# Attention of a fused attention and expert kernel laid out anew: pairs of heads staged side by side, 64x64 score products, one softmax instruction for four heads

## The chip, the cores and the metric

The kernel runs on one core of a Trainium2 chip. The core has five instruction queues that run side by side and each in its own order: TensorE (PE, matrix products and transposes through a product with the identity), VectorE (DVE), ScalarE (ACT), GpSimd (POOL) and SyncE (SP, which here only issues transfers). They wait for one another through semaphores. Transfers are carried out by 16 DMA engines. SBUF holds tiles of up to 128 partitions; PE writes to PSUM, and DVE or ACT copy from there ("eviction"). The metric is the device time of one execution in microseconds, the median over runs.

## What is computed

Banded attention with two masks, then a mixture of experts in which each token goes to one expert. Everything is float32.

```python
B, H, S, D = 8, 8, 576, 64
scores = q @ k.T / sqrt(D)                       # per batch and head, 576 x 576
rel = pos[:, None] - pos[None, :]
mask_plain = (rel >= 0) & (rel < 32)             # heads 0..3
mask_dil = (rel >= 0) & (rel < 128) & (rel % 4 == 0)   # heads 4..7
scores = where(mask, scores, -1e9)
attn = exp(scores - max) / (sum + 1e-9)
x = (attn @ v) as [4608 tokens, 512]
logits = x @ w_gate + modality_bias[modality_id]  # 8 experts
e = argmax(logits); gate = softmax(logits)[e]
out[token] = gate * (relu(x @ w1[e]) @ w2[e])     # w1 512 x 1024, w2 1024 x 512
```

## The kernel before

**Stages.** First the attention of all eight batches, with the routing of each batch worked in behind it; then the experts, in slots of 256 tokens of one expert. The change touches the attention alone.

**Units.** The attention is cut into tiles of 64 queries, which see 96 keys each. With the tokens of the dilated heads ordered by their class (position modulo 4), both masks are a band of 32 in that order, so both kinds of heads run through the same code: kind 0 are heads 0 to 3, kind 1 heads 4 to 7. A unit takes two tiles of one kind (the fifth unit of a batch one tile of each), that is, 2 tiles x 4 heads. A batch has 9 units and there are 72 in all, numbered t.

**One iteration of the loop.** The loop is software-pipelined, and PE, DVE, ACT and SP run it in the order in which it is written (`manual_schedule` over `MANUAL`); POOL's order is made by the scheduler. Iteration t emits:

1. `scores` of unit t: four products (lines 300 and 301). The queries of two heads lie as interleaved columns of `qT`, with zeros in the other head's 64 rows, so that one 128x128 by 128x96 product gives two heads of 64 queries. Then four times a DVE instruction (L305) that adds the mask and reduces the minimum (queries are stored negated, so the minimum is the maximum's negative; it shows as a custom instruction and a read of the accumulator), and four ACT exponentials (L308), with the minimum as the bias.
2. A piece of `qk_chunks` for keys of a coming half batch: four PE transposes (L257) of the loaded `kn` and two DVE evictions on 64 partitions each into `kT` (L272).
3. `attend` of unit t-2: eight PE products (L322) of the transposed probabilities `pT` and the values `vw`.
4. `logits` of unit t-4: small PE products (L360) of `uxh` and `uxl`, the two parts of the transposed output.
5. `normalize` of unit t-2 on DVE (L329, L330, L332, the last writing `x_sb`), and `gather_logits` of unit t-4 on DVE (L366, L371).
6. A piece of `qk_chunks` for queries: four PE transposes and two ACT evictions on 64 partitions into `qT` (L270).
7. `store` of unit t-3: two PE transposes of `x_sb` (L339), the ACT copy `uxh` (L343), the DVE difference `uxl` (L344), and the DMA of the rows to `x_dram` (L348, L352).
8. `probsT` of unit t-1: four PE transposes of the probabilities (L313), and the ACT eviction `pT` (L316).
9. One step of each task in `tasks`, above all the routing of the batch before (`gating`, from iteration 4 of the next batch on).

Pieces of step 2 and 6 come in eight of nine iterations of a batch: four for kind 0, four for kind 1.

**Routing on POOL.** `gating` uses POOL for small sums (L376 to L379, L416, L430, L432, L435, L437, operations on 96 partitions with at most 48 elements) and for six indirect DMAs per batch that scatter token numbers to the table of the experts (L442). From batch 6 on POOL also gathers rows of x for the first slots (L579), and for the first slot it computes six halves of the split of `w1` (L664).

**Loads.** SP issues the loads of a half batch (`load_qk`, then `load_v`) at iterations 0 and 4 of the batch before: keys and queries of four heads as 72 partitions with 8 successive tokens each, so that one packet has 2,048 bytes; values in packets of 256 bytes.

Of the kernel before, what the change touches and what calls it, by code (L numbers as in the profile page):

```python
# [10 lines left out]
F32 = mybir.dt.float32  # L11
# [14 lines left out]
NE = 8  # L26
# [7 lines left out]
SI = 8  # L34
PL = S // SI
# [26 lines left out]
def kernel(  # L62
# [21 lines left out]
    ps_s = ctx.enter_context(tc.tile_pool(name="ps_s", bufs=2, space=PSUM))  # L84
# [7 lines left out]
    # what the last batch's dilated units don't need lies where the experts can begin before those end  # L92
# [10 lines left out]
    for kd, pool in enumerate((aper0, aper)):  # L103
        qT.append(pool.tile([P, 2, S, 2], F32, name=f"qT{kd}"))
        kT.append(pool.tile([P, 2, WIN + S], F32, name=f"kT{kd}"))
    vw = [[pool.tile([KW, NTILE, 4, D + 1], F32, name=f"vw{kd}_{i}") for i, pool in enumerate((aperr, aper))] for kd in range(2)]

    def load_qk(b, kd):
        qn = ald.tile([PL, 4, SI, D], F32, name="qn")
        kn = ald.tile([PL, 4, SI, D], F32, name="kn")  # L110
        for g in (range(2) if b == 0 else (slice(0, 4),)):
            hs = g if isinstance(g, slice) else slice(2 * g, 2 * g + 2)
            for t, src in ((kn, k), (qn, q)):
                nc.sync.dma_start(out=t[:, hs], in_=src[b, 4 * kd + hs.start:4 * kd + hs.stop].rearrange("h (p si) d -> p h si d", si=SI))
# [25 lines left out]
    for kd in range(2):  # L140
        for a in range(2):
            (nc.gpsimd if kd else nc.vector).memset(qT[kd][a * D:(a + 1) * D, :, :, 1 - a], 0.0)
# [12 lines left out]
    # masks hold 0 where a key is seen and BIG elsewhere; rows are (query, head of the pair)  # L155
    MT = 6
    masks = cpool.tile([P, MT, KW], F32, name="masks")
    starts = [None, 0, CL - 2 * TQ, 2 * CL - 4 * TQ, 3 * CL - 6 * TQ, 3 * CL - 7 * TQ]
    nc.gpsimd.memset(masks, 0.0)
    for m, o in enumerate(starts):  # L160
        mt = masks[:, m, :]
        nc.gpsimd.affine_select(out=mt, in_=mt, pattern=[[2, KW]], compare_op=ALU.is_ge,
                                fill=BIG, base=-1, channel_multiplier=-1)
        nc.gpsimd.affine_select(out=mt, in_=mt, pattern=[[-2, KW]], compare_op=ALU.is_ge,
                                fill=BIG, base=2 * WIN, channel_multiplier=1)
        if o is not None:
            mo = masks[:, m, 0:WIN + o]
            nc.gpsimd.affine_select(out=mo, in_=mo, pattern=[[0, WIN + o]], compare_op=ALU.is_ge,
                                    fill=BIG, base=2 * o - 1, channel_multiplier=-1)
# [4 lines left out]
    # gate weights, modality terms, ids  # L174
# [20 lines left out]
    def constants():  # L195
        """What the routing needs, in pieces to be put between the first units."""
# [52 lines left out]
    def qk_chunks(kd, qn, kn):  # L249
        """The transposes of one half's keys and queries, as pieces to be put between units."""  # L250
        def chunk(h, is_q):
            src = qn if is_q else kn
            g, a = h // 2, h % 2
            pt = ps_t.tile([P, 512], F32, name="pt")
            ptv = pt[:, 0:4 * PL].rearrange("c (s p) -> c s p", p=PL)
            for s in range(4):
                nc.tensor.transpose(out=ptv[:, s, :], in_=src[:, h, 2 * s:2 * s + 2].rearrange("p u d -> p (u d)"),  # L257
# [642 lines left out]
```

## Time and profile before

| | |
|---|---|
| runs (three) | 791.31, 795.54, 800.52 us, median 795.54 |
| span of the profiled execution | 801.4 us, 5.9 us above the median of the runs |
| attention, normalisations of unit 0 to unit 71 | 23.3 to 336.4 us |
| mean granted TensorE clock | 0.940 |

The profile page gives the busy time of each engine, and groups of instructions by source line, with the mean duration of one and the idle time ahead of it with what ended it. The trace behind it answers further questions: the instructions in order of time, or the busy time of each engine between any two moments. "x4" in a row means that four like instructions were merged. A line number such as L305 is that of the kernel before; those of the changed kernel are 1 to 7 off, and each is given with its name.

### The profile page before, as it was taken

The page shows a single profiled execution, that of the slowest core. Times are in us where ns is not written, and L with a number is a line of the kernel's source. Part 1 is how long each engine was busy: PE and PEld are TensorE (multiplying, and loading weights), DVE is VectorE, ACT ScalarE, POOL GpSimd, SP SyncE. Part 2 cuts the span into 40 slices and gives each one's busy share as a digit, 9 for nine tenths or more (in the row PEclk, how much of TensorE's full clock was granted, in tenths as well). Part 3 has the DMA queues.
Part 4 walks back from the last instruction along what each step waited for, and adds up shares of the span by engine and source line. Part 5 has one row for each costly group of instructions (what it writes and reads, how often), then busy time and mean ns, then how long its engine had stood idle before and what let it go on. Part 6 is the DMA issues. An engine that isn't in the chain of part 4 may idle for free. (4 is left out here: it accounts for less than half of the span.)

```text
span 801.4 us, 16980 instructions
## 1 busy us (share of the span) xinstructions
PE 708.6 (88%) x5769; PEld 639.2 (80%) x5769; DVE 537.9 (67%) x1586; ACT 475.0 (59%) x933; POOL 350.6 (44%) x444
## 2 busy tenths in 40 slices
PE   7688888888882779999999988999999999699984
PEld 5688888888782768988889877988899999598963
DVE  5488888878883467687667744777666677457641
ACT  5588888788783349564366624656555456335641
POOL 5100314131235127577776524565556665156600
PEclk7799999999997579999999997999999999989998
DMA  8779777687836673102111261111111112611350
GB/s 164 166 173 179 163 140 143 148 150 155 146 81 142 159 178 79 40 2 54 55 28 47 75 194 53 46 47 48 51 54 54 41 41 89 191 51 53 115 155 24
DMA packets 97959, 79.63 MB, mean 99 GB/s; under 512 B 68443, under 2 KB 77707, under 8 KB 97870
## 3 DMA queue, kind: packets, MB, share of 16 engines
q1 hardware_dynamic: 88638, 59.32, 33.1%
q0 software_dynamic: 9232, 19.19, 8.4%
q8 instruction: 47, 0.77, 0.5%
q14 instruction: 42, 0.34, 0.2%
HBM read 122.15 MB, written 19.51 MB: 177 GB/s over the span
## 5 line engine op out<-in xcount | busy, mean ns | idle before, releaser
L579 POOL DMA_INDIRECT xg<-x_dram,gi x148 | 171.8, 1161 | 46.0 <-issue 39.7
L683 PE MATMUL pt<-xh,w1h 128*128 128x256 f32 x576 | 166.9, 290 | 10.6 <-ACT w1h L662 10.0
L683 PE MATMUL pt<-xh,w1l 128*128 128x256 f32 x576 | 167.4, 291 | 7.1 <-DVE w1l L664 7.1
L683 PE MATMUL pt<-xl,w1h 128*128 128x256 f32 x576 | 165.4, 287 | 0.0
L683 PEld LDWEIGHTS pt<-xh,w1h 128*128 128x128 f32 x576 | 113.1, 196 | 12.5 <-ACT w1h L662 10.6
L683 PEld LDWEIGHTS pt<-xh,w1l 128*128 128x128 f32 x576 | 112.8, 196 | 10.5 <-DVE w1l L664 10.3
L723 PE MATMUL po<-w2l,hh 128*128 128x512 f32 x296 | 117.6, 397 | 0.0
L723 PE MATMUL po<-w2h,hh 128*128 128x512 f32 x296 | 117.6, 397 | 0.0
L723 PE MATMUL po<-w2h,hl 128*128 128x512 f32 x296 | 117.4, 397 | 0.0
L674 ACT ACTIVATE hh<-pt 128x256 fp32r<-128x256 f32 x144 | 53.2, 383 | 108.2 <-PE pt L683 107.9
L270 ACT ACTIVATE qT<-pt 64x288 f32<-64x288 f32 x128 | 86.0, 672 | 51.4 <-PE pt L257 46.9
L683 PEld LDWEIGHTS pt<-xl,w1h 128*128 128x128 f32 x576 | 113.0, 196 | 0.8
L675 DVE SCALAR_TENSOR_TENSOR hl<-pt,hh 128x256 fp32r<-128x256 f32 x144 | 58.1, 421 | 78.8 <-ACT hh L674 78.6
L308 ACT ACTIVATE pe<-sm,nmx 128x96 f32<-128x96 f32 x288 | 84.6, 364 | 35.9 <-DVE nmx L305 35.1
L322 PE MATMUL po<-vw,pT 96*64 96x65 f32 x1152 | 75.4, 237 | 29.5 <-ACT pT L316 28.8
L664 DVE TENSOR_TENSOR w1l<-w1r,w1h 128x1024 fp32r<-128x1024 f32 (+1 forms) x74 | 85.0, 1204 | 20.6 <-ACT w1h L662 20.6
L322 PEld LDWEIGHTS po<-vw,pT 96*64 96x64 f32 x1152 | 65.2, 145 | 39.2 <-ACT pT L316 35.3
L272 DVE COPY kT<-pt 64x288 f32<-64x288 f32 x128 | 73.3, 572 | 28.4 <-PE pt L257 26.5
L662 ACT CAST w1h<-w1r 128x1024 fp32r<-128x1024 f32 (+1 forms) x80 | 76.9, 1003 | 21.1 <-DMA w1r<-in_moe_w_dram 11.4
L664 DVE TENSOR_TENSOR w2l<-w2r,w2h 128x1024 fp32r<-128x1024 f32 x76 | 88.6, 1220 | 0.6 <-ACT w2h L662 0.3
L300 PE MATMUL pss<-kT,qT 128*128 128x96 f32 x576 | 81.8, 288 | 1.3 <-ACT qT L270 1.3
L727 POOL DMA_INDIRECT out_dram<-ys,idt x37 | 39.1, 1056 | 91.6 <-issue 32.8
(175 smaller groups left out, 1224.2 us busy)
## 6 DMA issues: line engine op xcount, KB each, us to landing
w1r<-in_moe_w_dram SPq DMA_DIRECT2D x76, 512.0 KB
w2r<-in_moe_w_dram SPq DMA_DIRECT2D x76, 512.0 KB
kn<-in_k_dram SPq DMA_DIRECT2D x14, 576.0 KB
qn<-in_q_dram SPq DMA_DIRECT2D x14, 576.0 KB
vw<-in_v_dram SPq DMA_DIRECT2D x32, 192.0 KB
x_dram<-x_sb SPq DMA_DIRECT2D x40, 128.0 KB
vw<-in_v_dram SPq DMA_DIRECT2D x32, 96.0 KB
xg<-x_dram,gi POOLq DMA_INDIRECT x148, 3.3
```

Of the source, the lines that this page charges most:

```text
L270: nc.scalar.mul(dst, inp, -1.0 / 8.0)
L272: nc.vector.tensor_copy(out=dst, in_=inp)
L300: nc.tensor.matmul(out=ssv[:, j, :], lhsT=qT[kd][:, g, TQ * i:TQ * (i + 1), :].rearrange("p t a -> p (t a)"), rhs=kT[kd][:, g, TQ * i:TQ * ...
L308: nc.scalar.activation(out=self.pe[:, j, :], in_=sm[:, j, :], func=AF.Exp, bias=nmx[:, j:j + 1], scale=-1.0)
L322: nc.tensor.matmul(out=pov[u * TQ:(u + 1) * TQ, h, :], lhsT=self.pT[:, 2 * u + h // 2, h % 2::2], rhs=self.vts[kd][:, i, h, :], start=True ...
L579: load = nc.gpsimd.indirect_dma_start(out=xg[:, g, :], out_offset=None, in_=rows, in_offset=bass.IndirectOffsetOnAxis(ap=gi[:, g:g + 1], a ...
L662: (hi_eng.copy if hi_eng is nc.scalar else hi_eng.tensor_copy)(out=hi[cut], in_=raw[cut])
L664: lo_eng.tensor_tensor(out=lo[cut], in0=raw[cut], in1=hi[cut].bitcast(F32), op=ALU.subtract)
L674: nc.scalar.activation(out=hh[:, f, :], in_=ph, func=AF.Relu)
L675: nc.vector.scalar_tensor_tensor(out=hl[:, f, :], in0=ph, scalar=0.0, in1=hh[:, f, :].bitcast(F32), op0=ALU.max, op1=ALU.subtract)
L683: nc.tensor.matmul(out=ph, lhsT=wt[:, fs], rhs=xt[:, c, :], start=(c + n == 0), stop=(c + n == KC + 1))
L723: nc.tensor.matmul(out=py, lhsT=ht[:, f, ts_], rhs=wt[:, f % 2, :], start=(f + n == 0), stop=(f + n == FC + 1))
```

## The change

It rewrites how the attention's operands are staged, with the rest of the loop in its order:

- **Loads.** `load_qk` puts two heads side by side: partition p (48 of them per pair of heads, 96 for the two pairs) holds tokens 48 s + p, each as 64 numbers of one head beside 64 of the other. That makes eight DMAs per half batch in place of two, each of one head, in runs of 64 numbers (256 bytes). For kind 1 the class order is made here, by the load.
- **Transposes and evictions.** A piece now has three transposes of 96x128 in place of four of 72x128, and one eviction on 128 partitions of 2 x 144 elements, contiguous in the destination, in place of two on 64 partitions with strided destinations. Queries are evicted by ACT as before; keys of kind 0 by DVE, keys of kind 1 now by ACT.
- **Scores.** `qT` has no zeros and no interleaving any more. Eight products of 64 rows by 64 columns with 96 keys, each for one tile and one head, in place of four of 128x128. They go to the four quarters (two halves of the rows, two of the output's partitions) in turn, and to two banks of PSUM. The pool of these tiles has one buffer of two banks, in place of two of one bank.
- **Softmax.** One DVE addition of the mask for all four heads (384 elements per partition), one DVE maximum, one POOL subtraction of the maximum, one ACT exponential. Masks now hold the large negative number, five combinations of two tiles.
- **attend** reads the probabilities of each head as 128 successive columns, and alternates between the two tiles.

```diff
@@ load_qk
-        qn = ald.tile([PL, 4, SI, D], F32, name="qn")
-        kn = ald.tile([PL, 4, SI, D], F32, name="kn")
-        for g in (range(2) if b == 0 else (slice(0, 4),)):
...
+        qn = ald.tile([2 * PQ, SI, 2, D], F32, name="qn")
+        kn = ald.tile([2 * PQ, SI, 2, D], F32, name="kn")
+        for t, src in ((kn, k), (qn, q)):
+            for g in range(2):
+                for a in range(2):
+                    head = src[b, 4 * kd + 2 * g + a]
+                    dst = t[PQ * g:PQ * (g + 1), :, a]
+                    if kd == 0:
+                        nc.sync.dma_start(out=dst, in_=head.rearrange("(s p) d -> p s d", p=PQ))
...
@@ qk_chunks
+            for i in range(3):
+                nc.tensor.transpose(out=pt[:, 2 * PQ * i:2 * PQ * (i + 1)], in_=src[:, 3 * n + i].rearrange("p a d -> p (a d)"),
+                                    identity=ident[:2 * PQ, :2 * PQ])
...
+            if is_q:
+                nc.scalar.mul(dst, inp, 1.0 / 8.0)
+            elif kd == 0:
+                nc.vector.tensor_copy(out=dst, in_=inp)
+            else:
+                nc.scalar.copy(out=dst, in_=inp)
@@ Unit.scores
-            for u, (kd, i) in enumerate(self.jobs):
-                for g in range(2):
-                    j = 2 * u + g
-                    nc.vector.tensor_tensor_reduce(out=sm[:, j, :], in0=ssv[:, j, :], in1=masks[:, mask_of(kd, i), :],
-                                                   scale=1.0, scalar=3.0e38, op0=ALU.add, op1=ALU.min,
-                                                   accum_out=nmx[:, j:j + 1])
-                    nc.scalar.activation(out=self.pe[:, j, :], in_=sm[:, j, :], func=AF.Exp, bias=nmx[:, j:j + 1], scale=-1.0)
+            for g in range(2):
+                for u, (kd, i) in enumerate(self.jobs):
+                    for a in range(2):
+                        rows = slice(a * D, (a + 1) * D)
+                        nc.tensor.matmul(out=pss[u * TQ:(u + 1) * TQ, a, KW * g:KW * (g + 1)], lhsT=qT[kd][rows, g, TQ * i:TQ * (i + 1)],
+                                         rhs=kT[kd][rows, g, TQ * i:TQ * i + KW], start=True, stop=True)
...
+            nc.vector.tensor_reduce(out=nmx[:, :, 0], in_=sm, op=ALU.max, axis=AX.X)
+            nc.gpsimd.tensor_tensor(out=sm, in0=sm, in1=nmx.broadcast_to([P, 4, KW]), op=ALU.subtract)
+            nc.scalar.activation(out=self.pe, in_=sm, func=AF.Exp)
```

How the queues read now is seen at three places. The first is DVE in one iteration with a piece of kind 0; before, the rows of the softmax stand four times, of which the last pair is shown.

```order
L305 ISA sm,nmx<-pss,masks 128x96
L305 ISA nmx 128x1
L272 COPY kT_99<-pt 64x4x72 x2
L329 TENSOR_SCALAR den<-po 128x4
L330 RECIPROCAL den<-den 128x4
L332 TENSOR_TENSOR x_sb<-po,den 128x256
L366 COPY lT<-po 16x128
L344 TENSOR_TENSOR uxl<-pt,uxh 128x256
```

The same iteration of the changed kernel:

```order
L305 TENSOR_TENSOR sm<-pss,masks 128x2x2x96
L308 TENSOR_REDUCE nmx<-sm 128x4
L271 COPY kT_99<-pt 128x2x144
L331 TENSOR_SCALAR den<-po 128x4
L332 RECIPROCAL den<-den 128x4
L334 TENSOR_TENSOR x_sb<-po,den 128x256
L368 COPY lT<-po 16x128
L346 TENSOR_TENSOR uxl<-pt,uxh 128x256
```

The softmax is now two rows over all four heads and the key eviction one; both still follow the `uxl` of the iteration before, which waits for ACT.

The second place is ACT, in the iteration with the routing's exponential (`ex`) and into the next; before:

```order
L270 ACTIVATE qT_98<-pt 64x4x72 x2
L343 CAST uxh<-pt 128x256
L316 COPY pT<-pt 96x512
L414 ACTIVATE ex<-ex 96x48
L308 ACTIVATE pe<-sm,nmx 128x96 x4
L270 ACTIVATE qT_100<-pt 64x2x2x72 x2
```

And of the changed kernel:

```order
L269 ACTIVATE qT_98<-pt 128x2x144
L345 CAST uxh<-pt 128x256
L318 COPY pT<-pt 96x512
L416 ACTIVATE ex<-ex 96x48
L310 ACTIVATE pe<-sm 128x384
L273 COPY kT_101<-pt 128x2x144
L269 ACTIVATE qT_100<-pt 128x2x144
```

The exponential is one row, still ahead of the eviction of the queries and of `uxh` and `pT`, and the key eviction of kind 1 has come in behind it.

The third is POOL at the end of a batch's routing, with the scatter to the table (`table`); before:

```order
L435 TENSOR_TENSOR t_2190<-t_2190,oh 96x48
L376 TENSOR_TENSOR dstf_2194<-t_2190 96x24
L377 TENSOR_TENSOR dstf_2194<-dstf_2194 96x12
L379 TENSOR_TENSOR dstf<-dstf_2194 96x6
L437 CAST dst<-dstf 96x6
L442 DMA table<-pay,dst 41472x2 x6
L406 TENSOR_TENSOR ex<-l,mx 96x48
```

And of the changed kernel:

```order
L437 TENSOR_TENSOR t_2138<-t_2138,oh 96x48
L378 TENSOR_TENSOR dstf_2142<-t_2138 96x24
L379 TENSOR_TENSOR dstf_2142<-dstf_2142 96x12
L381 TENSOR_TENSOR dstf<-dstf_2142 96x6
L439 CAST dst<-dstf 96x6
L309 TENSOR_TENSOR sm<-sm,nmx 128x384
L444 DMA table<-pay,dst 41472x2 x6
L309 TENSOR_TENSOR sm<-sm,nmx 128x384 x4
```

The softmax's subtraction (L309) of each unit now stands between the routing's rows (as it does in each iteration), and all six scatters of a batch lie between the subtractions of two successive units.

More of the change, by code (lines that the diff above doesn't have):

```diff
@@ L33 @@
 KW = TQ + WIN
-SI = 8
-PL = S // SI
+PQ = 48
+SI = S // PQ
 GB = 96
@@ L108, in load_qk @@
     def load_qk(b, kd):
[L109 to L114 removed]
+        qn = ald.tile([2 * PQ, SI, 2, D], F32, name="qn")
[8 more added lines that the diff above has]
+                    else:
+                        nc.sync.dma_start(out=dst.rearrange("p (r k) d -> p r k d", r=NCLS), in_=head.rearrange("(k p r) d -> p r k d", p=PQ, r=NCLS))
         return qn, kn
@@ new lines, in scores @@
+            m = kinds.index(tuple(mask_of(*job) for job in self.jobs))
+            nc.vector.tensor_tensor(out=sm.rearrange("p (g a) w -> p a g w", a=2),
+                                    in0=pss[:, :, 0:2 * KW].rearrange("p a (g w) -> p a g w", w=KW),
+                                    in1=masks[:, m, :].rearrange("p (a g w) -> p a g w", a=1, g=1).broadcast_to([P, 2, 2, KW]), op=ALU.add)
+            nc.vector.tensor_reduce(out=nmx[:, :, 0], in_=sm, op=ALU.max, axis=AX.X)
+            nc.gpsimd.tensor_tensor(out=sm, in0=sm, in1=nmx.broadcast_to([P, 4, KW]), op=ALU.subtract)
```

78 lines of the change are left out of this document (29 added, 49 removed).

## The prediction

> **What bounds the kernel now.** I read the page first, then the busy times batch by batch, then the order of time within one iteration, then POOL's order of time. The change touches only the attention, so I cut the attention where the last unit of each batch is normalised (starts of L332), nine units to a row:
>
> ```profile
> span 801.4 us, 16980 instructions
> ...
> core 0: us, PE busy (x) PEld busy (x) DVE busy (x) ACT busy (x) POOL busy (x), PEclk, DMA share, GB/s
> 61.24:96.17 34.93, 30.76 (x391) 28.78 (x389) 29.51 (x146) 29.29 (x72) 4.26 (x16) 1.00 0.81 173
> 96.17:130.96 34.79, 30.64 (x390) 28.61 (x388) 29.52 (x146) 29.18 (x72) 9.00 (x22) 1.00 0.78 150
> 130.96:168.02 37.06, 32.24 (x390) 30.08 (x389) 29.48 (x145) 29.15 (x72) 8.82 (x21) 0.95 0.75 151
> 168.02:202.80 34.78, 30.65 (x389) 28.63 (x388) 29.53 (x145) 29.16 (x72) 8.83 (x21) 1.00 0.73 144
> 202.80:239.04 36.24, 31.41 (x396) 28.97 (x395) 31.75 (x164) 28.62 (x72) 11.54 (x27) 1.00 0.58 107
> 239.04:305.26 66.22, 42.39 (x389) 39.37 (x388) 31.98 (x148) 29.86 (x73) 20.35 (x36) 0.69 0.69 161
> 305.26:336.38 31.12, 29.70 (x354) 27.68 (x353) 23.75 (x121) 23.66 (x63) 20.54 (x31) 1.00 0.23 47
> ```
>
> PE, DVE and ACT are each busy 29 to 31 of 35 us, none is full, and POOL is nearly idle. So a loop through several engines sets the pace. The order of time of one iteration (kind 0) shows it, from one `uxh` to the next:
>
> ```profile
> 152.43 1.03 PE L300 MATMUL pss<-kT,qT 128*128 128x96 f32 x8
> ...
> 153.33 0.37 ACT L343 CAST uxh<-pt 128x256 fp32r<-128x256 f32 x1
> 153.60 0.58 ACT L316 COPY pT<-pt 96x512 f32<-96x512 f32 x1
> 153.74 0.42 DVE L344 TENSOR_TENSOR uxl<-pt,uxh 128x256 fp32r<-128x256 f32 x1 [0.28 <-ACT uxh L343]
> 154.08 0.25 DVE L305 CUSTOM_DVE_ANT_0 sm<-pss,masks 128x96 f32<-128x96 f32 x1
> ...
> 154.24 0.99 PE L322 MATMUL po<-vw,pT 96*64 96x65 f32 x16 [0.52 <-ACT pT L316]
> ...
> 154.43 1.17 ACT L308 ACTIVATE pe<-sm,nmx 128x96 f32<-128x96 f32 x4 [0.24 <-DVE nmx L305]
> ...
> 155.86 1.33 ACT L270 ACTIVATE qT<-pt 64x288 f32<-64x288 f32 x2 [0.26 <-PE pt L257]
> ...
> 157.22 0.37 ACT L343 CAST uxh<-pt 128x256 fp32r<-128x256 f32 x1
> ```
>
> `uxl` waits for `uxh` on ACT; the next softmax stands behind `uxl` on DVE; the exponentials wait for DVE; the query eviction and the next `uxh` stand behind them on ACT. Its terms: `uxh` to `uxl` 0.41, to the first mask 0.34, to the first exponential 0.35, to the eviction 1.43, to the next `uxh` 1.36: 3.89 us, nine of them 35.0.
>
> **The parts of the change.** Durations for the new instructions come from these groups:
>
> ```profile
> L270 ACT ACTIVATE qT<-pt 64x288 f32<-64x288 f32 x128 | 86.0, 672 | 51.4 <-PE pt L257 46.9 <-PE po L394 1.9 <-PE pt L339 0.7
> L272 DVE COPY kT<-pt 64x288 f32<-64x288 f32 x128 | 73.3, 572 | 28.4 <-PE pt L257 26.5
> L332 DVE TENSOR_TENSOR x_sb<-po,den 128x256 f32<-128x256 f32 x72 | 30.6, 425 | 2.7 <-DVE den L330 0.3
> L399 DVE TENSOR_REDUCE mx<-l 96x6 f32<-96x48 f32 x8 | 1.9, 235 | 0.3
> L396 DVE TENSOR_TENSOR l<-po,mterm 96x48 f32<-96x48 f32 x8 | 1.6, 194 | 0.6 <-PE po L394 0.6
> L218 POOL TENSOR_TENSOR mterm<-mterm,mtmp 96x384 f32<-96x384 f32 x1 | 1.0, 1005 | 0.1
> L216 POOL TENSOR_TENSOR mtmp<-mid_f,bias_sb 96x384 f32<-96x384 f32 x1 | 0.8, 826 | 17.2 <-DVE mid_f L209 17.2
> ```
>
> - *Softmax.* DVE additions out of PSUM take 0.194 us at 48 elements and 0.425 at 256, 1.11 ns each, so 0.57 at 384; the maximum, 0.235 at 48, comes to 0.60 at the same slope. POOL has the very shape: 0.826 to 1.005 us, and I take 0.93. ACT takes 0.37 us for 256 elements (`uxh`) and 0.58 for 512 (`pT`), so 0.48 for 384; it starts the next about 0.1 before an instruction's end (0.27 from `uxh` to `pT`), so 0.38 counts. From mask to eviction: 0.57 + 0.04, 0.60 + 0.08 to POOL, 0.93 + 0.08 to ACT (hand-overs as the 0.04 from `uxh` to `uxl`, doubled where POOL takes part), 0.38: 2.68 us, where it was 0.35 + 1.43 = 1.78.
> - *Evictions.* Queries: one of 288 elements, contiguous, 0.40 by the same ACT slope, 0.30 counted, where the pair took 1.36. Keys of kind 1 add another 0.30 on ACT ahead of it; before they ran on DVE beside the loop.
> - *The loop* is then 0.41 + 0.34 + 2.68 + 0.30 = 3.73 us with a piece of kind 0, 4.03 of kind 1, 3.43 with none: 4 x 3.73 + 4 x 4.03 + 3.43 = 34.5 us per batch against the 34.9 measured. What the evictions save, the two passes on DVE and the step over POOL take back: -0.4.
> - *Scores on PE*, unseen in this form. From above: 16 passes at the pace of `attend`'s 16 (about 0.99 us for 65 columns, so 1.46 for 96) in place of 1.03, +0.4; from below, four at a time, -0.7. Either way PE's 30.8 us per batch stay under the loop. The transposes, three in place of four, and the alternating `attend` lie there too, and count nothing while the loop covers them. One buffer of scores suffices, since the mask addition that frees it ends over 1 us before the next scores.
> - *What POOL already does* now delays the subtraction behind it, and nothing in the loop has room for that:
>
> ```profile
> 229.29 0.23 POOL L376 TENSOR_TENSOR sume<-ex 96x24 f32<-96x24 f32 x1 [7.05 <-ACT ex L414]
> ...
> 230.79 0.75 POOL L432 TENSOR_TENSOR run<-run,r 96x8 bf16<-96x8 bf16 x3
> ...
> 241.30 0.97 POOL L442 DMA_INDIRECT table<-pay,dst  x1 [0.28 <-DVE uxl L344]
> 242.57 0.93 POOL L442 DMA_INDIRECT table<-pay,dst  x1 [0.30 <-issue]
> ...
> 247.47 0.92 POOL L442 DMA_INDIRECT table<-pay,dst  x1 [0.30 <-issue]
> 248.70 0.99 POOL L579 DMA_INDIRECT xg<-x_dram,gi  x1 [0.30 <-issue]
> ```
>
> The six scatters hold POOL 7.1 us. They start when DVE has finished an iteration, and the next subtraction would be ready 1.2 us later (mask and maximum), so each batch's scatter costs 5.9. The eight sums from 229.29 to 231.54 start with the same iteration's end and cost 2.25 - 1.2, the later five some 0.6: 1.7. Ends: nothing, if the lag of the later steps absorbed it; 9.4, if none of it lay beside the softmax.
> - *Sum.* Five full batches (1 to 5): -0.4 and +1.7 each, four scatters: +30. Batch 6 took 66.2 us instead of 34.9 because PE stood waiting for keys behind the first weights:
>
> ```profile
> 264.86 0.71 PE L257 MATMUL pt<-ident,kn 72*128 72x72 f32 x4 [16.83 <-DMA kn<-in_k_dram]
> ```
>
> There eleven gathers now stand between subtractions, 1.27 us from one to the next, less 1.2 twice for the softmax beside them: +11.6. With the scatter and the sums that is +19, which runs down the wait rather than adding to it: I take 62 us, -4, between 50 and 76. Batch 7 has no pieces, and its middle units (five of them in this row of the busy times) take 2.9 us,
>
> ```profile
> 313.00:327.64 14.64, 14.62 (x182) 13.53 (x181) 12.66 (x73) 13.80 (x40) 11.52 (x18) 1.00 0.32 60
> ```
>
> and the split of `w1` on POOL has this group:
>
> ```profile
> L664 POOL TENSOR_TENSOR w1l<-w1r,w1h 128x512 fp32r<-128x512 f32 x6 | 7.5, 1270 | 1.2 <-ACT w1h L662 1.2
> ```
>
> They become 3.43 (+5 over the batch); the scatter (+5.9), the sums (+1.7), four gathers (+3) and the six halves of the split of `w1`, up to two of them at a time between subtractions (+3), make +18 in all. The start stays bound by loads (0, bounds -3 and +10). Together +44 on the span of 801.4, so 845; the median of the runs stands 5.9 below that execution, so 840.
> - *Loads.* Keys and queries go from 576 packets of 2,048 bytes per half batch to 4,608 of 256. With work queued up, packets of 256 bytes move like this (queues from 14 to 18 us):
>
> ```profile
> DMA packets 2332, 0.67 MB, mean 166 GB/s; under 512 B 2286, under 2 KB 2286, under 8 KB 2332
> ```
>
> At 571 packets per us, 4,608 and the 3,328 of the values take 13.9 us per half batch, 27.8 per batch, and 1.18 MB of stores at the same 166 GB/s 7.1: 34.9, inside the 42 that the loop now takes. So I count nothing, and the cover is thin only if the loop is faster than I think. The Trainium skill (DMA: Bandwidth & Descriptors, Specifications) puts the smallest transfer for full rate at 512 bytes and says that below it the engine reads, modifies and writes; by that these loads would be slow, as the values' packets already are. The trace agrees as far as it goes: the 166 GB/s are those of 256-byte packets, so the sum already pays that price, and by the rule it stays 840 while the loop covers the loads.
>
> **The rivals.**
>
> *Loads become the bound* (slower still). When the pieces of the values for kind 1 are issued, packets move at 432 per us:
>
> ```profile
> DMA packets 3025, 0.75 MB, mean 108 GB/s; under 512 B 3023, under 2 KB 3023, under 8 KB 3023
> ```
>
> If eight small DMAs do no better, a batch needs 2 x 18.4 + 7.1 = 43.9 us, batches 1 to 5 +8.5 each, batch 6 with 4 MB of weights +4, the start +13, batch 7 +10: 865. For it: the DMA share is already 0.73 to 0.81. Against it: that stretch (20 to 27 us) had little queued. By its rule of 512 bytes the Trainium skill (the same section) would point here; no row before the change has keys in such packets.
>
> *Faster.* If the exponential's wait for POOL is covered, the loop is gone: ACT falls by (86.0 - 64 x 0.40 + 72 x 1.17 - 72 x 0.48 - 32 x 0.40)/8 = 12 us per batch, DVE by 3, and PE's 31 us are the bound. Then batches 1 to 5 gain 3.5 each, and batch 6, whose wait for loads stays, nothing: 778. It decides if the subtraction is ready before ACT asks. Against it: ACT's queue has the exponential of unit t ahead of everything else of iteration t, and the wait of 0.24 us on DVE is there already with a shorter chain.
>
> *No change.* The POOL delays come, but batch 6 gives back nearly all of its wait (50 us instead of 62, -12), the lag absorbs half of the six scatters (-18), and the subtraction takes 0.83 us (72 x 0.1, -7): 803.
>
> **Chances.** Forecast 0.66, loads 0.12, faster 0.12, no change 0.10. The likeliest is 840. With the bounds of POOL's delays (sub 0.83 to 1.0: -7 to +5; scatters half hidden: -18; batch 6: -12 to +14; start: -3 to +10) and the loads' rival inside, 8 in 10 lie between 806 and 876; the faster case is left out. The kernel's runs differ by about 1%, so smaller changes can't be told: slower by over 1% 0.79, within 0.09, faster 0.12.
>
> **What would show it.** Right: after 96 us the batches take 41 to 43 us; ACT's largest idle time stands ahead of the exponential with POOL named; POOL's idle time shrinks; one iteration per batch of some 9 us, with the six scatters in it; the query eviction near 0.40 us. Wrong: PE waiting for `kn` or `qn` in batches 1 to 5 (loads), PE without gaps (faster), a subtraction far from 0.93 us, or batches near 35 us with scatters between the subtractions.

## The result, and the profile after

| | before | after |
|---|---|---|
| median of four runs | 794.07 us (791.31 to 800.52) | 840.12 us (838.66 to 842.19) |
| ratio after to before, 95% interval | | 1.0568 (1.0507 to 1.0629) |
| profiled span | 801.4 us | 840.5 us |
| mean granted TensorE clock | 0.940 | 0.887 |

The changed kernel is slower by 5.7%. Taken again in a later series, it took 843.43 us beside 793.75 (ratio 1.0623, 1.0570 to 1.0676). The kernel before took 846 to 851 us in the series of experiments 1 to 4 and 9 to 11, and 794 to 796 in all others, so totals below are compared inside a series only, and across series single batches are compared.

The first view is the busy time of each engine after, batch by batch, cut where the last unit of each batch is normalised (starts of L334), as for the kernel before. The columns are the stretch, its length, and the busy time and number of instructions of each engine.

```profile
span 840.5 us, 17288 instructions
...
core 0: us, PE busy (x) PEld busy (x) DVE busy (x) ACT busy (x) POOL busy (x), PEclk, DMA share, GB/s
60.69:96.60 35.91, 27.44 (x443) 22.11 (x441) 24.46 (x79) 15.06 (x40) 11.40 (x25) 0.93 0.95 159
96.60:139.24 42.64, 31.29 (x448) 25.29 (x447) 24.74 (x80) 15.17 (x40) 15.92 (x31) 0.82 1.03 152
139.24:182.33 43.09, 29.27 (x446) 23.81 (x444) 24.48 (x79) 15.17 (x40) 16.22 (x31) 0.84 0.75 127
182.33:225.07 42.74, 28.44 (x444) 23.02 (x442) 24.56 (x79) 15.17 (x40) 16.18 (x31) 0.88 0.78 125
225.07:269.81 44.74, 30.79 (x451) 24.67 (x450) 26.59 (x98) 15.06 (x40) 16.35 (x34) 0.81 0.46 95
269.81:329.06 59.25, 35.92 (x448) 29.07 (x447) 26.99 (x82) 16.01 (x41) 30.34 (x47) 0.69 0.77 166
329.06:377.65 48.59, 33.99 (x410) 28.44 (x408) 24.60 (x77) 17.85 (x43) 26.64 (x40) 0.72 0.14 34
```

ACT's busy time fell from 29 to 15 us per batch and DVE's from 29.5 to 24.5, and yet the batches grew from 35 to 43 us. No engine is above 75% busy from the second row on: a loop sets the pace here too. The difference by stage is 209.1 - 177.8 = +31.3 us in the first five rows, -7.0 in batch 6 (66.22 before), +17.5 in batch 7 (31.12 before), -0.6 at the start, -2.2 behind the attention: +39.1, the difference of the spans. (The profiled execution of before lay above its median, so the medians are 46 apart.)

The second view is the order of time of the changed loop, one turn of it with a piece of kind 0.

```profile
161.01 0.55 DVE L308 TENSOR_REDUCE nmx<-sm 128x4 f32<-128x384 f32 x1
161.71 0.82 POOL L309 TENSOR_TENSOR sm<-sm,nmx 128x384 f32<-128x384 f32 x1 [0.84 <-DVE nmx L308]
...
161.83 0.56 PE L302 MATMUL pss<-kT,qT 64*64 64x96 f32 x16
162.56 0.52 ACT L310 ACTIVATE pe<-sm 128x384 f32<-128x384 f32 x1 [2.65 <-POOL sm L309]
162.99 0.39 ACT L269 ACTIVATE qT<-pt 128x288 f32<-128x288 f32 x1
163.28 0.36 ACT L345 CAST uxh<-pt 128x256 fp32r<-128x256 f32 x1
...
163.68 0.43 DVE L346 TENSOR_TENSOR uxl<-pt,uxh 128x256 fp32r<-128x256 f32 x1 [0.83 <-ACT uxh L345]
164.13 0.55 DVE L305 TENSOR_TENSOR sm<-pss,masks 128x384 f32<-128x384 f32 x1
```

From maximum to subtraction 0.70 us, to the exponential 0.85, to the query eviction 0.43, to `uxh` 0.29, to `uxl` 0.40, to the mask addition 0.45, and 0.59 from there to the maximum (164.13 to 164.72): 3.71 us, DVE, POOL, ACT, DVE, each waiting for the one before. ACT stands idle 2.65 us of it, for POOL.

The third view is the iteration with the six scatters, POOL, DVE and the exponential alone.

```profile
94.33 0.18 DVE L441 RECIPROCAL pay<-sume 96x6 f32<-96x6 f32 x1
94.43 0.51 DVE L305 TENSOR_TENSOR sm<-pss,masks 128x384 f32<-128x384 f32 x1
94.98 0.55 DVE L308 TENSOR_REDUCE nmx<-sm 128x4 f32<-128x384 f32 x1
95.47 1.16 POOL L444 DMA_INDIRECT table<-pay,dst  x1 [2.93 <-issue]
...
101.84 0.92 POOL L444 DMA_INDIRECT table<-pay,dst  x1 [0.30 <-issue]
102.78 0.84 POOL L309 TENSOR_TENSOR sm<-sm,nmx 128x384 f32<-128x384 f32 x1
103.65 0.52 ACT L310 ACTIVATE pe<-sm 128x384 f32<-128x384 f32 x1 [9.22 <-POOL sm L309]
```

The maximum is done at 95.53, the subtraction starts at 102.78, behind the last scatter: 7.25 us later. ACT is idle 9.22 us, PE and DVE behind it. The next normalisation comes 11.08 us after the one at 96.60; in the following batches 11.37, 11.35 and 11.37.

The groups of instructions by source line show the sizes (mean duration of one in ns after the busy total; idle time of the engine ahead of it last):

```profile
L309 POOL TENSOR_TENSOR sm<-sm,nmx 128x384 f32<-128x384 f32 x72 | 59.5, 827 | 110.2 <-DVE nmx L308 95.1 <-DVE den L331 14.8
L308 DVE TENSOR_REDUCE nmx<-sm 128x4 f32<-128x384 f32 x72 | 39.8, 553 | 2.5
L305 DVE TENSOR_TENSOR sm<-pss,masks 128x384 f32<-128x384 f32 x72 | 39.3, 546 | 8.7 <-PE pss L302 8.5
L310 ACT ACTIVATE pe<-sm 128x384 f32<-128x384 f32 x72 | 37.6, 523 | 218.5 <-POOL sm L309 218.5
L269 ACT ACTIVATE qT<-pt 128x288 f32<-128x288 f32 x64 | 25.8, 404 | 17.7 <-PE pt L263 17.7
```

All of ACT's 218.5 us of idle time ahead of the exponential ends with POOL's subtraction.

### The profile page after: what moved, and what is told of

The parts are those of the page before. It is cut to its first block, busy times and chain, and to the rows that moved or that the text cites. A ratio compares the mean times of both kernels' runs of the same rounds, so it can differ in the third digit from the quotient of the medians.

```text
span 840.5 us, 17288 instructions
## 1 busy us (share of the span) xinstructions
PE 691.1 (82%) x6217; PEld 593.2 (71%) x6217; DVE 496.5 (59%) x1056; ACT 364.2 (43%) x685; POOL 407.3 (48%) x522
## 5 line engine op out<-in xcount | busy, mean ns | idle before, releaser
L581 POOL DMA_INDIRECT xg<-x_dram,gi x148 | 166.0, 1121 | 45.5 <-issue 36.6
L310 ACT ACTIVATE pe<-sm 128x384 f32<-128x384 f32 x72 | 37.6, 523 | 218.5 <-POOL sm L309 218.5
L685 PEld LDWEIGHTS pt<-xh,w1l 128*128 128x128 f32 x576 | 111.1, 193 | 13.3 <-DVE w1l L666 13.3
L309 POOL TENSOR_TENSOR sm<-sm,nmx 128x384 f32<-128x384 f32 x72 | 59.5, 827 | 110.2 <-DVE nmx L308 95.1
L685 PEld LDWEIGHTS pt<-xl,w1h 128*128 128x128 f32 x576 | 111.1, 193 | 0.7
L346 DVE TENSOR_TENSOR uxl<-pt,uxh 128x256 fp32r<-128x256 f32 x72 | 30.5, 424 | 114.4 <-ACT uxh L345 114.4
L324 PE MATMUL po<-vw,pT 96*64 96x65 f32 x1152 | 58.5, 254 | 40.5 <-ACT pT L318 39.8
L263 PE MATMUL pt<-ident,kn 96*128 96x96 f32 x192 | 35.5, 304 | 62.8 <-ACT kT L273 42.0
L729 POOL DMA_INDIRECT out_dram<-ys,idt x37 | 42.7, 1153 | 91.5 <-ACT xh L648 34.6
L324 PEld LDWEIGHTS po<-vw,pT 96*64 96x64 f32 x1152 | 47.5, 161 | 55.2 <-ACT pT L318 51.6
```

The source lines that it names most:

```text
L263: nc.tensor.transpose(out=pt[:, 2 * PQ * i:2 * PQ * (i + 1)], in_=src[:, 3 * n + i].rearrange("p a d -> p (a d)"), identity=ident[:2 * PQ, ...
L309: nc.gpsimd.tensor_tensor(out=sm, in0=sm, in1=nmx.broadcast_to([P, 4, KW]), op=ALU.subtract)
L310: nc.scalar.activation(out=self.pe, in_=sm, func=AF.Exp)
L324: nc.tensor.matmul(out=pov[u * TQ:(u + 1) * TQ, h, :], lhsT=self.pT[:, h, u * TQ:(u + 1) * TQ], rhs=self.vts[kd][:, i, h, :], start=True, ...
L581: load = nc.gpsimd.indirect_dma_start(out=xg[:, g, :], out_offset=None, in_=rows, in_offset=bass.IndirectOffsetOnAxis(ap=gi[:, g:g + 1], a ...
L685: nc.tensor.matmul(out=ph, lhsT=wt[:, fs], rhs=xt[:, c, :], start=(c + n == 0), stop=(c + n == KC + 1))
```

## The experiments

The theory: the softmax passes POOL, so each turn of the loop is as long as before, and all other work of POOL stands in it. The rivals: the loads in 256-byte packets set the pace; or the place of POOL's work does not matter, only its amount. Experiments 1 to 4 are one series, 5 to 8 the next, then 9 to 11, then 12.

**1. The subtraction on VectorE.**

```diff
-            nc.gpsimd.tensor_tensor(out=sm, in0=sm, in1=nmx.broadcast_to([P, 4, KW]), op=ALU.subtract)
+            nc.vector.tensor_tensor(out=sm, in0=sm, in1=nmx.broadcast_to([P, 4, KW]), op=ALU.subtract)
```

> The kernel after, with the one subtraction per unit (L309) on VectorE instead of POOL; nothing else differs. Theory (the loop of uxl, mask addition, maximum, subtraction and exponential passes POOL, and everything else POOL does delays it): the scatters, routing sums and gathers leave the path, so batches 2 to 5 fall from 42.6-44.7 us to 33-36, the iterations with six scatters from 11.1-11.4 us to about 4, batch 7 from 48.6 to 33-38, and the time is 785 to 805. Rival 1 (the loads are the bound of batches 2 to 5): those batches stay at 40 us or more, PE waits for kn or qn, time 825 or more. Rival 2 (VectorE becomes the bound, since it is given a fourth pass of about 0.5 us per unit): batches 36 to 39, VectorE busy over 90% in them, time 805 to 825.

Measured: 842.29 us beside 850.59 of the kernel before (0.9893, 0.9855 to 0.9932). Its first three batches (columns as above):

```profile
63.15:94.93 31.78, 25.86 (x448) 20.87 (x451) 28.71 (x88) 15.08 (x41) 4.98 (x16) 1.00 0.88 155
94.93:131.54 36.61, 29.41 (x447) 22.94 (x451) 28.97 (x88) 15.30 (x41) 9.60 (x22) 0.91 0.87 146
131.54:172.68 41.14, 35.74 (x447) 28.14 (x451) 29.86 (x89) 16.28 (x41) 9.40 (x21) 0.71 0.95 150
```

One instruction on another queue takes 4 us from the first batch (35.91 in the kernel after) and 6 from the second, and the turns of the first batch take 3.3 to 3.9 us in place of 3.5 to 4.9, though DVE is given more: 28.7 us of 31.8. About half of the 4 us is the instruction itself, 0.58 us on DVE and 0.83 on POOL, nine times. That the loop goes through POOL holds. The expected times did not come: the total is not 785 to 805 us, and batches 2 to 5 take 36.6 to 42.7 and not 33 to 36. The iteration after each batch's end still takes about 8 us, though POOL is out of the loop (experiments 9 to 11 come back to it), and the later batches stay well above the first.

**2. The scatters in parts.**

```diff
             scatters.append(ins)
+            if c % 2 == 1 and c < NGB - 1 and b < B - 1:
+                state['pool'] = ins
+                yield
```

> The kernel after, with the six scatters of a batch issued two, two and two in three successive iterations, in place of all six in one; the last batch is as it was. Theory (a scatter block holds up the next subtraction by its length less the slack of one iteration, about 2.7 us): two scatters hold POOL about 2.5 us and fit, or nearly, between two subtractions, so the iteration of 11.1-11.4 us goes, three iterations grow by at most 1.3 us each, batches 1 to 5 fall by 4 to 7 us each, and the time falls by 20 to 30, to 810 to 820. Rival (what costs the time is POOL's total work or the loads, not its place): the time stays within 5 us of 840.

Measured: 854.35 us beside 850.59 (1.0052, 1.0027 to 1.0078). The scheduler put them on POOL as three and three rather than two, two, two. Batches 2 and 3:

```profile
98.25:137.76 39.51, 28.41 (x443) 22.93 (x441) 24.57 (x79) 15.06 (x40) 16.62 (x31) 0.90 0.89 146
137.76:176.88 39.12, 29.74 (x448) 24.01 (x447) 24.41 (x79) 15.06 (x40) 16.11 (x31) 0.88 0.87 150
```

Against 42.64 and 43.09 (42.81 and 43.02 in experiment 4, of the same series) this is 3.1 and 4.0 us less for the same work of POOL (16 us in either). In the kernel after, the subtractions around the six scatters start 11.06 us apart, and the next one 3.90 later. Here they start 7.39 us apart around the first three scatters and 4.38 around the other three, which follow a subtraction at once: those fit beside the softmax but for 0.5 us. So the place counts, not the amount. The gain per batch is at or under the low end of the 4 to 7 us expected, since the first block held three; the total is not the 810 to 820 expected, and the kernel after was not run in this series to set it against.

**3. The old softmax in the new layout.**

```diff
...
-            nc.vector.tensor_reduce(out=nmx[:, :, 0], in_=sm, op=ALU.max, axis=AX.X)
-            nc.gpsimd.tensor_tensor(out=sm, in0=sm, in1=nmx.broadcast_to([P, 4, KW]), op=ALU.subtract)
-            nc.scalar.activation(out=self.pe, in_=sm, func=AF.Exp)
+            for h in range(4):
+                nc.vector.tensor_tensor_reduce(out=sm[:, h, :], in0=pss[:, h % 2, KW * (h // 2):KW * (h // 2 + 1)], in1=masks[:, m, :],
+                                               scale=1.0, scalar=3.0e38, op0=ALU.add, op1=ALU.min,
+                                               accum_out=nmx[:, h, :])
+                nc.scalar.activation(out=self.pe[:, h, :], in_=sm[:, h, :], func=AF.Exp, bias=nmx[:, h, :], scale=-1.0)
```

> The kernel after, with the softmax of the kernel before (four mask-and-minimum instructions on VectorE and four exponentials with a bias on ScalarE per unit; masks and the query factor with the sign that it needs); the staging of two heads, the 128-partition evictions and the 64x64 scores stay. Theory (of the four parts of the change only the softmax over POOL costs time, and the evictions and scores save some): the loop is 0.41 + 0.34 + 0.35 + 1.43 + 0.30 = 2.83 us, POOL is out of it, and batches 2 to 5 fall from 42.6-44.7 us to 29-35 us; batch 6 stays at its wait for loads; time 765 to 795, at or under that of the kernel before. Rival (loads in packets of 256 bytes are the bound once the loop is fast): batches 2 to 5 end at 35 to 40 us with PE waiting for kn or qn, time 790 to 820.

Measured: 838.15 us beside 850.59 (0.9864, 0.9838 to 0.9890). Undisturbed turns take mostly 2.5 to 2.8 us (2.83 were worked out), but the batches vary from 29.5 to 45.3 us, and the total lies above what theory and rival expected. The loop is fast and something else holds the batches.

**4. No later loads of queries and keys.** The staged tiles of the first batch are used again for all others; the loads themselves are left out.

```diff
-                    state['qk', b + 1, 0], state['v', b + 1, 0] = load_qk(b + 1, 0), load_v(b + 1, 0)
+                    state['qk', b + 1, 0], state['v', b + 1, 0] = state['qk', 0, 0], load_v(b + 1, 0)
...
```

> The kernel after without the loads of queries and keys of batches 2 to 7: the staged tiles of batch 1 are transposed again for each later batch (so the outputs are those of other inputs). Theory (loop through POOL is the bound, loads are hidden): batches 2 to 5 stay within 1.5 us of 42.6-44.7, batch 6 falls from 59 to 45-50 us since the wait for kn behind the weights goes; time 825 to 838. Rival (loads in packets of 256 bytes set the pace): batches 2 to 5 fall to 36 us or less, time 800 or less.

Measured: 854.72 us beside 850.59 (1.0055, 1.0021 to 1.0088).

```profile
92.92:135.73 42.81, 31.10 (x446) 25.17 (x445) 24.73 (x79) 15.17 (x40) 15.93 (x30) 0.82 0.32 69
135.73:178.75 43.02, 30.21 (x447) 24.46 (x446) 24.47 (x79) 15.17 (x40) 16.18 (x31) 0.81 0.31 69
```

The DMA share falls to 0.31 and batches 2 to 4 stay at 42.8 to 43.4 us, as in the kernel after with all its loads. In that kernel the loads are hidden. Unless two effects cancel, a batch held by POOL also takes the same time in this series as in that of the result. Batch 5 did not stay: it took 49.45 us (44.74 in the kernel after), with more of POOL's work in it (21.15 us in place of 16.35), and batch 6 took 51.01 (59.25); together they are 3.5 us shorter. The total is not the 825 to 838 expected; behind the attention this run took 483 us, where the kernel after took 463.

**5 and 6. Both kernels again**, unchanged, with experiments 7 and 8.

> The kernel before, unchanged, for its profile beside these runs: in the series of the first four experiments it took a median of 850.6 us, where it took 794.1 in the series of the result. From the last normalisation of the attention to the end those four experiments took 482 to 485 us, the kernels before and after 465.0 and 462.9. Theory 1 (the whole program is slower there by one factor): attention 336 x 485/465 = 351 us, total about 836. Theory 2 (the attention of before loses more, by waits for loads): attention 360 us or more, in batches with PE waiting for kn or qn, total about 850. If this series runs as that of the result did: 794.

> The kernel after, unchanged, timed beside these runs. Theory 1 (what slows the first four experiments slows both kernels alike): ratio to before 1.04 to 1.07 again. Theory 2 (the attention of after is held by POOL, so slower loads cost it little): attention 370 to 380 us as before, total 855 to 865 where before takes 850, ratio 1.00 to 1.02.

Measured: before 792.88 us in its one run, after 843.43 (ratio 1.0623). This series ran like that of the result, so it repeats the result and says nothing on the other series; how the kernel after runs in those was not tried.

**7. The old softmax without the later loads of queries and keys**, the third and the fourth edit together.

> The kernel of the third experiment (new staging, evictions and scores, old softmax) without the loads of queries and keys of batches 2 to 7: the staged tiles of batch 1 are transposed again (so the outputs are those of other inputs). Theory (with POOL out of the loop the loads in 256-byte packets are the bound, 35 us per batch by estimate, 37 measured on average in batches 1 to 5 of the third experiment): batches 2 to 5 fall to 26-30 us, the slow iterations after each batch go, the attention ends at 300 to 325 us, the time is 25 to 50 under the third experiment's. Rival (the slow iterations come from the scatters alone): they stay at 8 us or more, and the time falls by less than 15.

Measured: 724.18 us beside 793.75 (0.9122, 0.9057 to 0.9188).

```profile
51.86:77.06 25.20, 24.96 (x446) 20.78 (x444) 21.74 (x133) 21.67 (x68) 3.87 (x16) 1.00 0.57 127
77.06:102.29 25.23, 24.98 (x446) 20.78 (x444) 21.68 (x133) 21.39 (x68) 9.17 (x22) 1.00 0.55 117
```

PE is busy 24.96 of 25.20 us: with POOL out of the loop and the loads of queries and keys gone, PE is the bound, lower than its 30.8 us of before, since the 16 passes of the scores take 0.56 us (161.83 above) where the eight took 1.03, and `attend` 0.69 in place of 0.99. The iterations with the scatters take 2.8 to 3.0 us; experiment 8, with loads, shows 2.9 to 3.2 for most of them, so this series has no slow ones to explain. It also shows that without the step over POOL the same scatters cost the loop next to nothing. So the new evictions and scores are worth about 10 us per batch, if nothing else holds the loop.

**8. New queries, old keys**, the old softmax.

```diff
-        kn = ald.tile([2 * PQ, SI, 2, D], F32, name="kn")
+        kn = ald.tile([PL, 4, SK, D], F32, name="kn")
...
+            nc.sync.dma_start(out=kn[:, hs], in_=k[b, 4 * kd + hs.start:4 * kd + hs.stop].rearrange("h (p si) d -> p h si d", si=SK))
```

> A mixture that could beat both: the kernel of the third experiment with the keys staged as before (72 partitions, one transfer per half batch in packets of 2,048 bytes, four transposes and two evictions of 64 partitions per head; one of the two of kind 1 on ScalarE). Queries two heads side by side, 128-partition evictions, 64x64 scores and the old softmax stay. Theory: the queries' eviction leaves the loop (2.83 us against 3.89) and the packets of a batch fall from 15,900 to 11,800 (27 us at 571 per us), so batches 2 to 5 take 28 to 32 us and the time is 20 to 40 under the kernel before of the same series. Rival (VectorE with about 30 us per batch, or what still is in small packets, holds it): 33 to 36 us per batch, the time within 1% of before.

Measured: 806.96 us beside 793.75 (1.0152, 1.0098 to 1.0206). Its batches 2, 3 and 6:

```profile
97.32:134.49 37.17, 31.25 (x454) 25.76 (x452) 27.76 (x141) 23.25 (x68) 9.23 (x22) 0.82 0.90 143
134.49:172.09 37.60, 30.53 (x454) 25.25 (x452) 27.65 (x141) 23.28 (x69) 9.91 (x23) 0.82 0.83 144
240.77:318.67 77.90, 35.32 (x451) 29.26 (x449) 29.92 (x143) 24.25 (x69) 24.46 (x40) 0.64 0.67 142
```

Batches 4 and 5 take 34.60 and 34.08 us. So with a quarter of the packets gone batches 2 to 5 do not reach the 28 to 32 us of the theory; they lie at and above the 33 to 36 of the rival, and batches 1 to 5 together (177.7 us) are no shorter than in the kernel before of the same series (175.3). PE waited for queries (nine times, 15.6 us) and for keys (44.0 us, of which 40.6 in batch 6, behind the first weights). Batch 6 alone is 16.2 us longer than before (61.69) and accounts for the loss. No run of this series has the same buffers and all packets small, so what fewer packets are worth by themselves is not shown here.

**9 to 11. A third buffer for queries and keys; the third and the first experiment again.**

```diff
-    ald = rctx.enter_context(tc.tile_pool(name="ald", bufs=2, side="right"))
+    ald = rctx.enter_context(tc.tile_pool(name="ald", bufs=3, side="right"))
...
+                if b + 2 < B:
+                    state['qk', b + 2, 0] = load_qk(b + 2, 0)
...
```

> The kernel of the third experiment (new staging, evictions and scores, old softmax) with a third buffer for the staged queries and keys, so that each half batch is loaded half a batch earlier: at iteration 0 of a batch the kind-1 half of the next batch, at iteration 4 the kind-0 half of the batch after it; the value loads stay where they are. Theory (in the third experiment PE waited for loads that were issued only four or five iterations before their use, and a batch's transfers fit into about 28 us when their queue is never empty): batches 2 to 5 take 27 to 32 us, the wait for kn in batch 6 shrinks or goes, and the time is 740 to 775 where before takes 794. Rival (what the transfers can move per us is the bound, whatever the order): batches 2 to 5 stay at 35 to 38 us, the time at 785 to 810.

> The kernel of the third experiment once more, since the before beside it took 851 us then and 794 in the other series. Theory (loads held it there): batches 2 to 5 at 30 to 38 us here too, 785 to 810 where before takes 794. Rival (there the transfers were slow for a reason outside the kernel, and only that held it): batches of 26 to 29 us, 750 or less.

> The kernel of the first experiment once more (the subtraction on VectorE), for the same reason. Theory: POOL leaves the loop, typical iterations 3.1 to 3.4 us, batches 2 to 5 at 32 to 38 us with some waits for loads, time 785 to 810 where before takes 794 and after 840 to 843. Rival: batches of 40 us or more, time over 825.

Measured beside 846.32 of before: 826.66 (0.9766, 0.9740 to 0.9792), 835.98 (0.9883, 0.9820 to 0.9946) and 839.66 us (0.9918, 0.9884 to 0.9951). The last two repeat experiments 3 and 1. All three totals lie above what theory and rival expected, but for the eleventh's rival with its over 825 us; batches 2 to 5 take 32.6 to 39.4, 31.4 to 42.8 and 36.3 to 42.6 us. The iterations after each batch's end take 6.3 to 10.4 us in all three, and the busy times of the ninth show how, in steps of 2 us around the end of its scatters (93.21 to 100.50):

```profile
96.00:98.00 2.00, 0.41 (x3) 0.22 (x2) 0.34 (x2) 0.34 (x1) 1.70 (x2) 1.00 0.18 32
98.00:100.00 2.00, 0.00 (x0) 0.00 (x0) 1.18 (x4) 0.44 (x2) 1.39 (x3) 0.97 0.14 31
100.00:102.00 2.00, 0.00 (x0) 0.00 (x0) 0.00 (x0) 0.00 (x0) 0.49 (x1) 0.50 0.33 72
```

While POOL issues the last of its scatters, and for 1.5 us behind them, PE comes to a stop, DVE and ACT nearly so, and the transfers with them (share 0.14), though the subtraction is no longer POOL's. No row names a releaser that explains it, and its cause stays open. In the series of experiments 5 to 8 and 12 the same iterations of the seventh, eighth and twelfth take 2.5 to 3.2 us, one of them 3.7.

**12. The ninth with more buffers for the outputs**, `bufs=12` in place of 8 for `x_sb`.

> The kernel of the ninth experiment (old softmax, new staging, evictions and scores, three load buffers) with twelve instead of eight buffers for the normalised outputs, since VectorE stood 30.4 us in all ahead of x_sb there, waiting for stores. Theory if this series runs like that of the result (before 794): PE is no longer kept waiting by loads or stores, batches 2 to 5 take 27 to 32 us, the time is 740 to 775. Theory if it runs like the series of the ninth experiment (before 846): the waits of x_sb go, the pause behind each batch's scatters stays, 800 to 822. Rival in either: the waits for stores turn into waits for loads and the ratio to before stays at 0.97 to 1.00.

Measured: 789.31 us beside 795.51 (0.9920, 0.9888 to 0.9953), in a series like that of the result.

```profile
59.29:84.54 25.25, 24.98 (x446) 20.79 (x444) 21.84 (x134) 21.73 (x68) 3.88 (x16) 1.00 0.76 160
84.54:122.86 38.32, 30.46 (x446) 24.83 (x444) 22.33 (x134) 22.36 (x68) 9.15 (x22) 0.82 0.74 141
122.86:161.75 38.89, 34.34 (x448) 28.05 (x445) 22.65 (x134) 23.05 (x69) 9.55 (x23) 0.74 0.89 147
```

The first batch runs at PE's 25.2 us, since its data were loaded ahead; the next four take 37 to 39, and PE waits for them (84.54 to 235.57):

```profile
PE pt L263 <- DMA qn<-in_q_dram: 11.5, 6, 2.9
PE pt L263 <- DMA kn<-in_k_dram: 7.8, 2, 3.9
```

Behind these waits its granted clock is 0.74 to 0.82 on average, which makes its work longer too. So the rival of the expectation holds: the waits for stores became waits for loads. What makes the loads late is not settled. SP, whose queue issues them all, shows one issue behind the other:

```profile
110.82 5.45 SPq L130 DMA_DIRECT2D vw<-in_v_dram  x4
116.31 0.77 SPq L131 DMA_DIRECT2D vw<-in_v_dram  x1
117.18 3.53 SPq L353 DMA_DIRECT2D x_dram<-x_sb  x6
```

In batches 2 and 3 no pause between two issues of SP is longer than 0.4 us, where before it has pauses of up to 2.5 us; a batch now asks for 47 to 51 issues, where before it took 33 to 37. So the single queue that issues may be the bound as well as the DMA engines, whose share is 0.74 to 0.94. But single issues take up to 3.3 us (median 0.55), so the transfers may hold that queue in turn. Issuing a part of the loads from another queue was not tried.

Of the versions that compute everything it is the one that was faster than before in a series like that of the result, by 0.8%; against the kernel after it was not run side by side, but that took 1.057 to 1.062 times before. The gain is not in the batches that wait for loads: batches 2 to 5 take 151.0 us, where before they take 140.4 (experiment 5). It comes from the first batch (-9.6) and batch 6 (-5.4), less 5.1 lost in batch 7.

## Why the prediction was right

The forecast was 840 us and slower, and it came out so for the reason given: the step over POOL keeps the loop as long as it was, and what else POOL does stands in it. That the median is met to the microsecond is luck. On the span the forecast was +44 us and the two profiles differ by 39.1; the forecast then took off 5.9 us, by which the profiled execution of before lay above its median, and that of after (840.5) lies at its median. The second pair of profiles (experiments 5 and 6) splits as +32.7 in batches 1 to 5, -1.3 in batch 6, +17.4 in batch 7, +2.3 at the start and -0.2 behind the attention, +50.9 in all. By its steps:

- **The loop.** 3.73 us were forecast for a turn with a piece of kind 0; the turn shown takes 3.71. In it, 0.85 us from the subtraction to the exponential (1.01 forecast) is made up for by 0.45 from `uxl` to the mask addition (0.34), where an instruction of the routing stands in between, and 0.05 at the exponential. With the routing's sums the first full batch was forecast at 34.5 + 1.7 = 36.2 us and took 35.91. The durations: addition 0.546 us (0.57), maximum 0.553 (0.60), subtraction 0.827 (0.93), exponential 0.523 (0.48), query eviction 0.404 (0.40). Experiment 1 shows the path directly: off POOL, the same step on a fuller engine takes that batch to 31.8 us.
- **The scatters** were priced at 5.9 us per batch and cost 6.7 to 7.2 (batches 2 to 4 against the first). The mis-sized term is the sentence that they start when DVE has finished an iteration and that the subtraction would be ready 1.2 us later: the release is at 94.51, but the first scatter's record starts at 95.47, about when the maximum is ready. The view shows no work on POOL in that first microsecond, so it seems to hold POOL as well, and the slack was used up by it. Experiment 2 shows that their place makes the price, and experiments 7, 8 and 12 that it is paid through the softmax on POOL: without that, the same scatters stand in iterations of about 3 us. Batches 1 to 5 come to +31.3 us against +30, since before two of these batches had been 1.4 and 2.3 us longer than the others.
- **Batch 6**: -7.0 us against -4. The wait for `kn` behind the weights is run down, as said, from 16.83 us to 8.7. This batch varies from run to run, though: 66.22 and 61.69 us before, 59.25 and 60.36 after.
- **Batch 7**: +17.5 against +18. **The start**: -0.6 against 0. **Behind the attention**: -2.2, where nothing was forecast.
- **The loads count nothing**: right while POOL holds the loop (experiment 4), and the warning that the cover is thin was right as well. The 34.9 us for a batch's transfers were too few: with the loop fast, the batches that wait for them take 37 to 39 us (experiment 12). The rival that made them the bound had the place wrong for this kernel and the price, 43.9, too high.
- **The rival of a faster kernel** took PE's 31 us as the next bound. The runs show 25.2 for PE, and 34 to 39 where batches wait for loads. So without POOL in the loop the change would have come to about no difference: 0.977 to 0.992 of before in experiments 1, 3 and 9 to 12, each in its own series.

As for the rule of 512 bytes (the Trainium skill, DMA: Bandwidth & Descriptors, Specifications), the prediction read the trace as agreeing with it; set beside larger packets, the trace speaks against it as far as it goes. Here are the transfers of seven microseconds of before (123 to 130 us), in which 576 of the packets are its large ones, and then those of ten microseconds of after (61 to 71 us), all but one in small packets:

```profile
DMA packets 1354, 1.37 MB, mean 196 GB/s; under 512 B 778, under 2 KB 778, under 8 KB 1354
```

```profile
DMA packets 6965, 1.76 MB, mean 176 GB/s; under 512 B 6964, under 2 KB 6964, under 8 KB 6964
```

Small packets moved at nine tenths of the rate. In batches 2 to 4 of experiment 8, which has both kinds, a packet of 256 bytes took 18 ns and one of 2,048 bytes 135 ns (medians), about the same per byte; and the core moved 147 GB/s there and 146 in the same batches of experiment 12, which has a third more packets. Why a batch's 5.4 to 5.7 MB (38.32 us at 141 GB/s, 38.89 at 147) then took 37 to 39 us in experiment 12, and not the 31 to 33 of 176 GB/s, no run here settles.

## What to carry to other kernels

An engine that is idle three quarters of the time is no free place for a step of a tight loop: look at the longest block of other work on its queue, since the loop stops for that block less its slack, each time. Where blocks can't be moved, cut them to the slack. And when a loop is to become faster, price what lies under it first: here the gains in evictions and scores were real, 10 us per batch where no load was late, and late loads took them back (experiment 12).

## What the runs showed of the hardware that was not expected

- A wait costs PE twice. After the iteration with the scatters PE had no work for some microseconds, and its granted clock stood at 0.50 while it was busy again:

```profile
145.00:147.00 2.00, 0.00 (x0) 0.00 (x0) 0.00 (x0) 0.41 (x1) 1.53 (x2) 0.50 0.02 1
147.00:149.00 2.00, 1.25 (x13) 0.96 (x15) 0.96 (x3) 1.44 (x5) 0.00 (x0) 0.50 0.07 4
149.00:151.00 2.00, 2.00 (x22) 1.87 (x20) 1.20 (x5) 0.52 (x2) 0.82 (x1) 0.50 0.00 0
```

```profile
151.86 0.92 PE L302 MATMUL pss<-kT,qT 64*64 64x96 f32 x16
152.91 0.56 DVE L305 TENSOR_TENSOR sm<-pss,masks 128x384 f32<-128x384 f32 x1 [0.59 <-PE pss L302]
```

  The scores (the first row from the order of time) take 0.92 us just behind it and 0.56 at full clock. In batches 2 to 5 the mean clock was 0.81 to 0.88, where before it was mostly 1.00; in experiment 7, where PE hardly waits, it is 1.00. It was not in the sum. In most turns it is off the path while POOL holds the loop, but not in this one: the mask addition (the second row) waited 0.59 us for these scores. The Trainium skill (TensorE: Matmul & The Clock Gate, Part 1) describes such a gate, half rate after an idle window and full rate after some microseconds of work; the rows agree.
- In some series the whole core stood nearly still for some 5 us around the end of POOL's scatters (experiment 9), in others it did not. Whether the scatters cause it was not tried.
- The scores as 64x64 products, sent to the four quarters in turn, take half the time: 0.56 us for 16 passes, where eight passes of 128x128 took 1.03. That the quarters work side by side is a reading of this; no run changes it alone.
